# First batch's start-up order, spacing of the key/value loads, and the place of one PSUM copy in a fused attention and adapter kernel

## The chip, the cores and the metric

The kernel runs on one core of one Trainium2 chip. The metric is device time in microseconds (us) of one execution. Three timed runs of the kernel before gave 441.35, 442.04 and 440.4 us, median 441.35. One more execution was profiled; everything read from a profile below is from that one.

## What is computed

Four batches of 12288 query rows of 128 floats attend to a pooled key/value map. The map (384 x 32 positions) is averaged over 4 x 4 blocks, which gives 768 rows per batch, and multiplied by `w_sr`; keys and values are the same matrix. The attention output goes through a gated mixture of eight rank-16 adapters, of which the two with the largest logits count.

```python
kv_pool = kv.reshape(B, H // r, r, W // r, r, C).mean(axis=(2, 4))
k = v = kv_pool.reshape(B, -1, C) @ w_sr
a = softmax(scale * (q @ k.T));  x = a @ v
logits = x @ w_gate              # 8 experts, top 2, softmax over the two
out = x + sum_over_top2(w_e * ((x @ A_e) @ B_e))
```

## The kernel before, in words

**Tiling.** The 49152 query rows are 96 chunks of 512 (`NTOK`), 24 per batch (`CPB`), and four chunks form a group of 2048 rows (`GROWS`). The 768 key rows are six blocks of 128, loaded as three kv tiles per batch (`NT = 3`), each in four row parts of 512 KB.

**One order written by hand.** All instructions are emitted in program order under a manual schedule, and each engine executes its own in that order. The main loop (line 403) is a software pipeline over `c`. For the iteration `c` it emits, in this order: `scores(c+2, 0)` (TensorE product, ScalarE exponential), `gate_weights` every second iteration (ScalarE tanh, two GpSimd operations that end in `gw`), `weigh(c-1, 0)` (12 matmuls), `scores(c+2, 1)`, `up(c-5)` (four matmuls into `d_ps`, the VectorE sum `osb` at L333, and the store), `weigh(c-1, 1)`, `normalise(c-1)` (VectorE: `rinv_all`, `xn`, four MAX8 `top`), `gate` every second iteration (VectorE `msk`, GpSimd `m`, `arg`), `transposed(c-2, c-4)` (eight TensorE transposes into `t_ps`, and their copy `xh`, on VectorE at L311), `scores(c+2, 2)`, the batch preparation `prep`, `down(c-3)` (four matmuls into `h_ps`), and `apply_gate(c-3)` (the VectorE product `hg` at L322).

**What ties the steps together.** `up(c-4)` in iteration c+1 loads `hgT` as its weights, the second half of the copy `xh` of iteration c; and it writes `d_ps`, which shares its one PSUM buffer (`ps_h`, one buffer) with the `h_ps` that `hg` of iteration c reads. So `up` waits for both `xh` and `hg`. `osb` waits for `up`. `rinv_all` waits for the last matmul of `weigh`.

**Batch preparation.** While batch b runs, `prep(b+1, k)` prepares the next one, with k the chunk's number in its batch. It issues the loads of kv tile k on SP's queue at k = 0, 1, 2 (for the first batch k = 0 is emitted ahead of the loop). The pooling sums run on GpSimd at odd k from 3 to 13. At k = 16 the six pooled blocks are transposed (`kp_ps`) and copied to `kpT` (VectorE, L161), at k = 18 the keys are made (`k_ps`, copy `kfT`, L168), at k = 20 the values (`v_ps`, copy `vext`, L176), and at k = 21 two VectorE reductions run (L196, L198).

**Queues.** SP issues, in order: the kv loads (L83), the transposing loads `qT` of a query group (`load_q`, L230, every fourth iteration, at c = 2, 6, 10, ...) and one store per chunk (L335). GpSimd issues the casting copies `q_bf` (L90), one per group in the same iterations. They share the DMA engines.

**Start.** For the first group the queries are loaded as float32 (`q0`, L96) and transposed on TensorE in four blocks (L370), each copied by ScalarE to `qT[0]` (L372) with a stride, since a partition holds four neighbouring rows. Then, for each kv tile of batch 0: VectorE sums, two transposes, `kpT`, keys (L183, L184), values (L191, L193), and the scores of chunks 0, 1 and 2. The PSUM tiles of scores, transposes, keys and values rotate through two buffers (`ps_s`).

Of the kernel before, what the change touches and what calls it, by code (L numbers as in the profile page):

```python
# [11 lines left out]
BF16 = mybir.dt.bfloat16  # L12
# [3 lines left out]
AF = mybir.ActivationFunctionType  # L16
# [5 lines left out]
def kernel(  # L22
# [10 lines left out]
    nc = tc.nc  # L33
    P = 128
# [6 lines left out]
    NTOK = 512  # L41
    NS = NTOK // P
    VW = C + E + 1
    CPB = N // NTOK
    NCH = B * CPB
# [11 lines left out]
    run = ctx.enter_context(tc.tile_pool(name="run", bufs=3))  # L57
# [12 lines left out]
    qflat = q.rearrange("b n c -> (b n) c")  # L70
# [6 lines left out]
    NT = NJ // 2  # L77

    def load_kv(b, t):
        k = kvt[b, t] = kvpool.tile([P, 4, 2, 4 * C], FP32, tag="kvt", name="kvt")  # L80
        src = kv[b].rearrange("(t h d) (w e) c -> t d h w (e c)", t=NT, d=4, e=8)
        for d in range(4):
            nc.sync.dma_start(k[:, d].rearrange("p u c -> p (u c)"), src[t, d])  # L83

    GROWS = 2048
    LEAD = 2

    def cast_q(g):
        r = slice(g * GROWS, (g + 1) * GROWS)
        nc.gpsimd.dma_start(q_bf[r], qflat[r])  # L90

    q0 = kvpool.tile([P, GROWS // NTOK, NS, C], FP32, tag="kvt", name="q0")
    for t in range(NT):
        load_kv(0, t)
        if t == 0:
            nc.sync.dma_start(q0, qflat[0:GROWS].rearrange("(k p s) c -> p k s c", p=P, s=NS))  # L96

    w_in = const.tile([P, P], FP32)
    nc.scalar.dma_start(w_in, w_sr)
# [37 lines left out]
    def sum_row(b, t, d, eng):  # L137
        v = kvt[b, t]
        eng.tensor_tensor(v[:, 0], v[:, 0], v[:, d], op=ALU.add)  # L139

    def sum_cols(b, t, eng):
        v = kvt[b, t][:, 0]
        eng.tensor_tensor(v[:, :, 0:2 * C], v[:, :, 0:2 * C], v[:, :, 2 * C:4 * C], op=ALU.add)
        eng.tensor_tensor(v[:, :, 0:C], v[:, :, 0:C], v[:, :, C:2 * C], op=ALU.add)

    def stile(name):
        return ps_s.tile([P, 2, NTOK], FP32, tag="sg", name=name)
# [16 lines left out]
    def keys(b):  # L164
        t = stile("k_ps")
        for h in range(2):
            mm(t[:, h, 0:HK], w_sr_sb, kpT[b][:, h * HK:(h + 1) * HK], start=True, stop=True)
        nc.vector.tensor_copy(kfT[b].rearrange("c (h k) -> c h k", h=2), t[:, :, 0:HK])  # L168
# [10 lines left out]
    def keys_of(b, t):  # L179

        s = slice(2 * t * P, 2 * (t + 1) * P)
        k_ps = stile("k_ps")
        mm(k_ps[:, 0, 0:2 * P], w_sr_sb, kpT[b][:, s], start=True, stop=True)  # L183
        nc.scalar.activation(kfT[b][:, s], k_ps[:, 0, 0:2 * P], AF.Copy)  # L184
# [15 lines left out]

    def prep(b, k):

        if k < NT:
            load_kv(b, k)
        if k % 2 == 1 and 3 <= k < 3 + 4 * NT:
            t, h = divmod((k - 3) // 2, 2)
            if h == 0:
                sum_row(b, t, 1, nc.gpsimd)
                sum_row(b, t, 2, nc.gpsimd)
            else:  # L210
                sum_row(b, t, 3, nc.gpsimd)
                sum_cols(b, t, nc.gpsimd)
        if k == 16:
            pooled_transposed(b, range(NJ))
        elif k == 18:
            keys(b)
        elif k == 20:
            values(b)
        elif k == 21:
            ranges(b)  # L220


    qT = {}
    tt, xps, xpair, xn, gw, gin, xT, hg, hgT, hps = {}, {}, {}, {}, {}, {}, {}, {}, {}, {}
    garg, gmsk = {}, {}
    GRP = GROWS // NTOK

    def load_q(g):
        qT[g] = qpool.tile([P, GROWS], BF16, tag="qT", name="qT")
        nc.sync.dma_start(qT[g], q_bf[g * GROWS:(g + 1) * GROWS], transpose=True)  # L230

    def scores(c, r):
        b = c // CPB
        if r == 0:
            tt[c] = ttpool.tile([P, NJ, NTOK], F16, tag="tt", name="tt")
        qc = qT[c // GRP][:, (c % GRP) * NTOK:(c % GRP + 1) * NTOK]
        sg = stile("sg")
        for k in range(2):
            j = 2 * r + k
            mm(sg[:, k], kfT[b][:, j * P:(j + 1) * P], qc, start=True, stop=True)  # L240
        nc.scalar.activation(tt[c][:, 2 * r:2 * r + 2], sg, AF.Exp, bias=0.0, scale=scale)  # L241
# [50 lines left out]
    def transposed(cx, ch):  # L292

        t_ps = ps_t.tile([P, 2, NS, P], BF16, tag="tp", name="t_ps")
        todo = []
        if chunk_ok(cx):
            hi = xn[cx].bitcast(U16)[:, :, 1:2 * C:2].bitcast(BF16)
            todo += [(0, s, hi[:, s]) for s in range(NS)]
        if chunk_ok(ch):
            todo += [(1, s, hg[ch][:, s]) for s in range(NS)]  # L300
        if not todo:
            return
        for i, (k, s, src) in enumerate(todo):
            mm(t_ps[:, k, s], src, id_bf, is_transpose=True,  # L304
               start=(i == 0), stop=(i == len(todo) - 1), skip_group_check=True)
        xh = run.tile([P, 2, NS, P], BF16, tag="xh", name="xh")
        lo, hi_ = todo[0][0], todo[-1][0] + 1
        if cx >= NCH - 2:
            nc.scalar.activation(xh[:, lo:hi_], t_ps[:, lo:hi_], AF.Copy)
        else:  # L310
            nc.vector.tensor_copy(xh[:, lo:hi_], t_ps[:, lo:hi_])  # L311
        xT[cx], hgT[ch] = xh[:, 0], xh[:, 1]

    def down(c):
        hps[c] = mtile([P, NS, P], name="h_ps")
# [3 lines left out]
    def apply_gate(c):  # L319
        hg[c] = run.tile([P, NS, P], BF16, tag="hg", name="hg")  # L320
        g = gw[c // 2][:, (c % 2) * NS:(c % 2 + 1) * NS]
        nc.vector.tensor_tensor(  # L322
            hg[c].rearrange("p s (e r) -> p (s e) r", r=RK),
            hps[c].rearrange("p s (e r) -> p (s e) r", r=RK),
            g.rearrange("p s e -> p (s e)").unsqueeze(2).broadcast_to([P, NS * E, RK]),
            op=ALU.mult)
# [10 lines left out]
    def chunk_ok(c):  # L337
        return 0 <= c < NCH
# [25 lines left out]


    qT[0] = qpool.tile([P, GROWS], BF16, tag="qT", name="qT")
    for k in range(GRP):
        t = stile("q_ps")
        for i in range(NS):
            mm(t[:, 0, i * P:(i + 1) * P], q0[:, k, i], id_f32, is_transpose=True,  # L370
               start=(i == 0), stop=(i == NS - 1), skip_group_check=True)
        nc.scalar.activation(  # L372
            qT[0][:, k * NTOK:(k + 1) * NTOK].rearrange("c (p s) -> c s p", s=NS),
            t[:, 0].rearrange("c (s p) -> c s p", s=NS), AF.Copy)

    a_bf = const.tile([P, P], BF16)
    b_half = const.tile([P, P], FP32)
# [1 line left out]
    for t in range(NT):  # L379
        for d in range(1, 4):  # L380
            sum_row(0, t, d, nc.vector)
        sum_cols(0, t, nc.vector)
        pooled_transposed(0, [2 * t, 2 * t + 1])
        if t == 0:
            nc.vector.tensor_copy(a_bf, a_f)
            nc.vector.tensor_scalar(b_half, b_f, 0.5, None, op0=ALU.mult)
            nc.vector.tensor_copy(b_bf, b_half)
        if t == NT - 1:
            tick = const.tile([P, 1], FP32)
            nc.gpsimd.tensor_copy(tick, kvt[0, t][:, 1, 0, 0:1])  # L390
            for g in range(1, 4):
                cast_q(g)
        keys_of(0, t)
        scores(0, t)
        values_of(0, t)
        for c in range(1, LEAD + 1):
            scores(c, t)
    load_q(1)
    load_q(2)
    prep(1, 0)  # L400

    NQ = NCH // GRP
    for c in range(1, NCH + 5):
        b, k = divmod(c, CPB)
        cs = c + LEAD
        if cs < NCH:
            if cs % GRP == 0:
                g = cs // GRP
                if g + 2 < NQ:
                    load_q(g + 2)  # L410
                if g + 3 < NQ:
                    cast_q(g + 3)
            scores(cs, 0)
        if chunk_ok(c - 2) and (c - 2) % 2 == 1:
            gate_weights((c - 2) // 2)
        if chunk_ok(c - 1):
            weigh(c - 1, 0)
        if cs < NCH:
            scores(cs, 1)
        if chunk_ok(c - 5):  # L420
            up(c - 5)
        if chunk_ok(c - 1):
            weigh(c - 1, 1)
            normalise(c - 1)
            if (c - 1) % 2 == 1:
                gate((c - 1) // 2)
        transposed(c - 2, c - 4)
        if cs < NCH:
            scores(cs, 2)
        if c < NCH:  # L430
            if b + 1 < B:
                prep(b + 1, k)
            if c == 1:
                ranges(0)
        if chunk_ok(c - 3):
            down(c - 3)
            apply_gate(c - 3)
        if c == NCH + 1:
            direct_ok()

# [3 lines left out]
    with tc.If(bad_v != 0):  # L444
# [8 lines left out]
        for b in range(B):  # L453
            for h in range(2):
                s = slice(h * NKV // 2, (h + 1) * NKV // 2)
# [104 lines left out]
```

## Time and profile before

| what | value |
|---|---|
| timed runs, median | 441.35 us |
| the profiled execution, its own time | 444.76 us |
| its span, first to last instruction | 443.0 us |
| what lies around the span | 1.76 us |
| busy: TensorE matmul / VectorE / ScalarE / GpSimd | 385.4 / 345.6 / 294.9 / 165.8 us |
| mean granted TensorE clock | 0.974 |

The profile gives, for each group of instructions, how long they were busy, how long one took, and what ended the idle time before them. The chain of waits follows the last instruction back, at each step to what released it. The timeline lists start, duration, engine, line and names; a bracket gives the idle time of the engine before the row and its releaser. "PE" is TensorE's matmul, "PEld" its weight load, "DVE" VectorE, "ACT" ScalarE, "POOL" GpSimd, "SP" SyncE. "issue" is idle time for which the profile shows no releaser.

### The profile page before, as it was taken

To read this page: it belongs to the slowest core of one execution; us is meant where nothing else is said; L and a number is where in the kernel's file an instruction comes from. 1 tells how busy PE (TensorE), PEld (TensorE's weight loads), DVE (VectorE), ACT (ScalarE), POOL (GpSimd) and SP (SyncE) were. 2 spreads that over 40 slices of the span, in tenths; PEclk is the share of its full clock that TensorE was granted. 3 is DMA by queue.
4 is the path that set the end of the run, shared out by engine and by line. 5 is a ranking of instruction groups with operands and counts; after the bars stand their busy time and mean duration, and the time that the engine had idled before them with its cause. 6 is when DMAs were issued, how large, how long until landed. Compare 5 with 4: busy or idle time off the path is not lost.

```text
span 443.0 us, 11324 instructions
## 1 busy us (share of the span) xinstructions
PE 385.4 (87%) x4455; PEld 302.6 (68%) x4527; DVE 345.6 (78%) x967; ACT 294.9 (67%) x351; POOL 165.8 (37%) x317
## 2 busy tenths in 40 slices
PE   0678996999989999999989999999989999999742
PEld 0335774777867777777877777777877777777641
DVE  3473786588888888888888888888888888888882
ACT  1468875677667777776667777767667777777321
POOL 1100886461122678752121787832113121121210
PEclk9989999799999999999999999999999999999995
DMA  8999999764466999685388999677357444111112
GB/s 269 405 201 280 308 175 177 152 144 97 144 124 209 321 288 234 161 168 115 102 167 225 284 279 243 175 155 144 102 119 164 117 122 121 73 66 59 70 72 78
DMA packets 71372, 76.51 MB, mean 173 GB/s; under 512 B 51744, under 2 KB 52000, under 8 KB 70944
## 3 DMA queue, kind: packets, MB, share of 16 engines
q1 hardware_dynamic: 69104, 63.45, 52.6%
q0 software_dynamic: 736, 12.06, 15.9%
q8 instruction: 37, 0.61, 0.6%
q10 hardware_dynamic: 1472, 0.20, 0.3%
q14 instruction: 23, 0.19, 0.2%
HBM read 50.53 MB, written 37.22 MB: 198 GB/s over the span
## 4 chain that ended last, share of the span: by engine, by line
PE 60%; DVE 29%; issue 4%; ACT 3%; DMA 3%; SPq 1%; DVEq 0%; ACTq 0%
PE xps L250 22%; PE sg L240 15%; DVE xh L311 9%; DVE hg L322 9%; PE d_ps L331 8%; PE t_ps L304 7%; PE h_ps L317 6%; DVE xn L261 5%; DMA q<-in_q_dram 2%; DVE top L268 2%; ACT tt L241 2%; DVE rinv_all L257 1%; PE v_ps L174 1%; PE k_ps L183 1%; ACT qT L372 1%
## 5 line engine op out<-in xcount | busy, mean ns | idle before, releaser
L241 ACT ACTIVATE tt<-sg 128x1024 f16<-128x1024 f32 x288 | 280.7, 1023 | 107.2 <-PE sg L240 75.9
L250 PE MATMUL xps<-vext,tt 128*128 128x137 f16 x2304 | 171.7, 224 | 2.0 <-DVE xn L261 0.7
L250 PEld LDWEIGHTS <-tt 128*128 128x128 f16 x2304 | 154.8, 113 | 23.6 <-DVE xn L261 2.3
L240 PE MATMUL sg<-qT,kfT 128*128 128x512 bf16 x504 | 158.2, 386 | 8.0 <-issue 4.1
L333 DVE TENSOR_TENSOR osb<-d_ps,xn 128x512 f32<-128x512 f32 x96 | 66.4, 692 | 48.2 <-PE d_ps L331 48.2
L274 POOL TENSOR_TENSOR m<-top 128x8 f32<-128x8 f32 x48 | 11.4, 237 | 183.5 <-DVE top L268 183.5
L261 DVE TENSOR_TENSOR xn<-xps,rinv_all 128x548 f32<-128x548 f32 x96 | 69.9, 728 | 3.3
L322 DVE TENSOR_TENSOR hg<-h_ps,gw 128x512 bf16<-128x512 f32 x96 | 65.3, 680 | 5.0 <-PE h_ps L317 5.0
L139 POOL TENSOR_TENSOR kvt<-kvt 128x1024 f32<-128x1024 f32 x27 | 64.0, 2369 | 0.7
L331 PEld LDWEIGHTS <-xh 128*128 128x128 bf16 x384 | 29.6, 98 | 49.4 <-issue 35.0
L311 DVE COPY xh<-t_ps 128x1024 bf16<-128x1024 bf16 (+1 forms) x94 | 63.1, 672 | 0.0
L331 PE MATMUL d_ps<-b_bf,xh 128*128 128x128 bf16 x384 | 37.6, 221 | 20.1 <-DVE hg L322 19.2
L240 PEld LDWEIGHTS <-kfT 128*128 128x128 bf16 x576 | 45.6, 99 | 13.1 <-issue 9.4
L317 PEld LDWEIGHTS <-xh 128*128 128x128 bf16 x384 | 29.7, 99 | 21.8 <-issue 2.2
L317 PE MATMUL h_ps<-a_bf,xh 128*128 128x128 bf16 x384 | 37.5, 221 | 2.0 <-DVE osb L333 0.7
L268 DVE MAX8 top<-xn 128x8 f32<-128x8 f32 x384 | 35.9, 156 | 3.3
L304 PE MATMUL t_ps<-id_bf,hg 128*128 128x128 bf16 x384 | 37.6, 221 | 0.0
L304 PE MATMUL t_ps<-id_bf,xn 128*128 128x128 bf16 x384 | 37.1, 219 | 0.0
L289 POOL TENSOR_SCALAR th<-th 128x64 f32<-128x64 f32 x48 | 17.8, 370 | 48.9 <-ACT th L287 48.9
L257 DVE RECIPROCAL rinv_all<-xps 128x4 f32<-128x4 f32 x96 | 17.5, 183 | 13.4 <-PE xps L250 10.1
L304 PEld LDWEIGHTS <-xn 128*128 128x128 bf16 x384 | 26.0, 98 | 0.0
L304 PEld LDWEIGHTS <-hg 128*128 128x128 bf16 x384 | 25.9, 99 | 0.0
(67 smaller groups left out, 186.5 us busy)
## 6 DMA issues: line engine op xcount, KB each, us to landing
kvt<-in_kv_dram SPq DMA_DIRECT2D x48, 512.0 KB, 7.2
out_dram<-osb SPq DMA_DIRECT2D x96, 256.0 KB, 3.0
q_bf<-in_q_dram POOLq DMA_DIRECT2D x23, 512.0 KB, 6.8
q<-in_q_dram SPq DMA_DIRECT2D x1, 1024.0 KB, 9.7
qT<-q_bf SPq DMA_TRANSPOSE x23, 8.4
w_in<-in_w_sr_dram ACTq DMA_DIRECT2D x1, 64.0 KB, 1.8
a_f<-in_moe_A_dram ACTq DMA_DIRECT2D x1, 64.0 KB, 10.2
b_f<-in_moe_B_dram ACTq DMA_DIRECT2D x1, 64.0 KB, 10.7
```

Source lines behind the costliest of these rows:

```text
L139: eng.tensor_tensor(v[:, 0], v[:, 0], v[:, d], op=ALU.add)
L240: mm(sg[:, k], kfT[b][:, j * P:(j + 1) * P], qc, start=True, stop=True)
L241: nc.scalar.activation(tt[c][:, 2 * r:2 * r + 2], sg, AF.Exp, bias=0.0, scale=scale)
L250: mm(o, tt[c][:, j, s::NS], vext[b][:, j], start=(j == 0 and s % 2 == 0), stop=(j == NJ - 1 and s % 2 == 1), skip_group_check=True)
L261: nc.vector.tensor_tensor(xn[c].rearrange("p (b s) v -> p b s v", b=2), xv, ri.rearrange("p (b s) -> p b s", b=2).unsqueeze(3).broadcast_t ...
L268: nc.vector.max(gin[c // 2][:, (c % 2) * NS + s], xn[c][:, s, C:C + E])
L304: mm(t_ps[:, k, s], src, id_bf, is_transpose=True, start=(i == 0), stop=(i == len(todo) - 1), skip_group_check=True)
L311: nc.vector.tensor_copy(xh[:, lo:hi_], t_ps[:, lo:hi_])
L317: mm(hps[c][:, s], xT[c][:, s], a_bf, start=(s == 0), stop=(s == NS - 1))
L322: nc.vector.tensor_tensor(hg[c].rearrange("p s (e r) -> p (s e) r", r=RK), hps[c].rearrange("p s (e r) -> p (s e) r", r=RK), g.rearrange(" ...
L331: mm(d_ps[:, s], hgT[c][:, s], b_bf, start=(s == 0), stop=(s == NS - 1))
L333: nc.vector.tensor_tensor(osb, d_ps, xn[c][:, :, 0:C], op=ALU.add)
```

## The change

There are three parts. **Start:** `q0` is loaded with each partition holding rows 128 apart (2048 runs of 512 bytes in place of 512 runs of 2 KB), so that its copy to `qT[0]` is contiguous. The transposes of the first kv tile come before the query blocks, and each query block comes just ahead of the first scores that need it; the fourth comes after all three kv tiles. **Loads:** the kv loads of the next batch move from k = 0, 1, 2 to k = 2, 6, 10, their sums to k = 5 to 15, and the pooled transposes from k = 16 to k = 17; keys, values and reductions stay. **Gate product:** the copy `xh` is emitted at the end of the iteration, so that on VectorE it stands behind the `prep` copies and behind `hg`.

```diff
-            nc.sync.dma_start(q0, qflat[0:GROWS].rearrange("(k p s) c -> p k s c", p=P, s=NS))
+            nc.sync.dma_start(q0, qflat[0:GROWS].rearrange("(k s p) c -> p k s c", p=P, s=NS))
...
-        if k < NT:
-            load_kv(b, k)
-        if k % 2 == 1 and 3 <= k < 3 + 4 * NT:
...
-        if k == 16:
+        if k in (2, 6, 10):
+            load_kv(b, (k - 2) // 4)
+        if k in (5, 9, 13):
+            sum_row(b, (k - 5) // 4, 1, nc.gpsimd)
+            sum_row(b, (k - 5) // 4, 2, nc.gpsimd)
+        elif k in (7, 11, 15):
+            sum_row(b, (k - 7) // 4, 3, nc.gpsimd)
+            sum_cols(b, (k - 7) // 4, nc.gpsimd)
+        if k == 17:
             pooled_transposed(b, range(NJ))
...
-        xh = run.tile([P, 2, NS, P], BF16, tag="xh", name="xh")
...
+        def evacuate():
+            xh = run.tile([P, 2, NS, P], BF16, tag="xh", name="xh")
...
+        return evacuate
...
-        nc.scalar.activation(
-            qT[0][:, k * NTOK:(k + 1) * NTOK].rearrange("c (p s) -> c s p", s=NS),
-            t[:, 0].rearrange("c (s p) -> c s p", s=NS), AF.Copy)
+        nc.scalar.activation(qT[0][:, k * NTOK:(k + 1) * NTOK], t[:, 0], AF.Copy)
...
         keys_of(0, t)
+        if t == 0:
+            queries(0)
         scores(0, t)
         values_of(0, t)
         for c in range(1, LEAD + 1):
+            if t == 0:
+                queries(c)
             scores(c, t)
+    for k in range(LEAD + 1, GRP):
+        queries(k)
     load_q(1)
     load_q(2)
-    prep(1, 0)
...
-        transposed(c - 2, c - 4)
+        evacuate = transposed(c - 2, c - 4)
...
             down(c - 3)
             apply_gate(c - 3)
+        evacuate()
```

More of the change, by code (lines that the diff above doesn't have):

```diff
@@ L201, in prep @@
     def prep(b, k):
-        if k < NT:
-            load_kv(b, k)
-        if k % 2 == 1 and 3 <= k < 3 + 4 * NT:
[L206 to L212, printed above, removed]
-        if k == 16:
+        if k in (2, 6, 10):
[7 more added lines that the diff above has]
+        if k == 17:
             pooled_transposed(b, range(NJ))
@@ L301, in transposed @@
         if not todo:
-            return
+            return lambda: None
         for i, (k, s, src) in enumerate(todo):
@@ L305, in transposed @@
                start=(i == 0), stop=(i == len(todo) - 1), skip_group_check=True)
-        xh = run.tile([P, 2, NS, P], BF16, tag="xh", name="xh")
[L307 to L312, printed above, removed]
+        def evacuate():
+            xh = run.tile([P, 2, NS, P], BF16, tag="xh", name="xh")
+            lo, hi_ = todo[0][0], todo[-1][0] + 1
+            if cx >= NCH - 2:
+                nc.scalar.activation(xh[:, lo:hi_], t_ps[:, lo:hi_], AF.Copy)
+            else:
+                nc.vector.tensor_copy(xh[:, lo:hi_], t_ps[:, lo:hi_])
+            xT[cx], hgT[ch] = xh[:, 0], xh[:, 1]
+        return evacuate
     def down(c):
@@ L366, with queries @@
     qT[0] = qpool.tile([P, GROWS], BF16, tag="qT", name="qT")
-    for k in range(GRP):
+    def queries(k):
         t = stile("q_ps")
```

## The prediction

> **What bounds the kernel now.** I read the chain of waits first, then the groups, then the timeline of one ordinary iteration, and last the DMA view by stretches. From the page:
>
> ```profile
> PE 60%; DVE 29%; issue 4%; ACT 3%; DMA 3%; SPq 1%; DVEq 0%; ACTq 0%
> ...
> L333 DVE TENSOR_TENSOR osb<-d_ps,xn 128x512 f32<-128x512 f32 x96 | 66.4, 692 | 48.2 <-PE d_ps L331 48.2
> L322 DVE TENSOR_TENSOR hg<-h_ps,gw 128x512 bf16<-128x512 f32 x96 | 65.3, 680 | 5.0 <-PE h_ps L317 5.0
> ```
>
> The chain runs mostly over PE, but it is a loop of PE and DVE: DVE's only large idle time is 48.2 us ahead of `osb`, 0.47 us in each of some 95 iterations. The timeline of an iteration with a gate shows the loop (start, duration, engine):
>
> ```profile
> 96.23 0.23 DVE L278 TENSOR_TENSOR msk<-xn,top 128x64 f32<-128x64 f32 x1
> ...
> 96.37 0.69 DVE L311 COPY xh<-t_ps 128x1024 bf16<-128x1024 bf16 x1
> ...
> 96.97 0.68 DVE L322 TENSOR_TENSOR hg<-h_ps,gw 128x512 bf16<-128x512 f32 x1
> 97.12 0.10 PEld L331 LDWEIGHTS <-xh 128*128 128x128 bf16 x1
> ...
> 97.71 0.38 PE L331 MATMUL d_ps<-b_bf,xh 128*128 128x128 bf16 x4 [0.21 <-DVE hg L322]
> ...
> 98.13 0.69 DVE L333 TENSOR_TENSOR osb<-d_ps,xn 128x512 f32<-128x512 f32 x1 [0.47 <-PE d_ps L331]
> ```
>
> DVE runs `osb`, `rinv_all`, `xn`, `top`, (`msk`), `xh`, `hg` without a break, then waits 0.47 us for `up` (L331), which waits for it. The starts of `rinv_all` give the period: 94.84, 98.86, 102.60, that is 4.02 us with a gate and 3.74 without. **Whatever lengthens DVE's loop counts fully; whatever PE, ACT or POOL lose inside their slack counts nothing.**
>
> **Gate product first, ordinary iterations.** `up` needs `xh` (weights) and `hg` (PSUM buffer), so their order moves no end: the later one still releases `up`. But the later one is now the weights. Above, the first weight load starts at 97.12, 0.06 after `xh`, and is done long before `hg` ends; in the new order it comes after the last wait. The nearest row for an exposed load is a `weigh` whose weight load itself waited, beside one whose load ran ahead:
>
> ```profile
> 44.04 0.75 PEld L250 LDWEIGHTS <-tt 128*128 128x128 f16 x12 [0.44 <-DVE xn L261]
> 44.04 0.92 PE L250 MATMUL xps<-vext,tt 128*128 128x137 f16 x12
> ...
> 45.01 0.94 PEld L250 LDWEIGHTS <-tt 128*128 128x128 f16 x12
> ...
> 45.23 0.89 PE L250 MATMUL xps<-vext,tt 128*128 128x137 f16 x12
> ```
>
> From the release to the last matmul's end 0.92 against 0.89: 0.03 us. Of the 96 `up`, some 92 follow a DVE copy: 92 x 0.031 = **+2.9 us**. Bounds: -0.9 (a weight load started 0.05 after its release, a matmul 0.06) and +9.0 (92 x 0.098, the mean L331 load in full). I take the row's own 0.03. `hg` now needs `h_ps` 0.6 us sooner, and has it: in that stretch `h_ps` (95.52, 0.39) ends at 95.91 and `msk` at 96.46; without a gate the slack is 0.29 us (99.53 + 0.39 = 99.92 against `top`'s end at 100.21). `gw` ends at 98.67, over a microsecond ahead of the 100.13 at which `hg` would want it.
>
> [...]
>
> **Gate product first, preparation iterations.** Here `xh` covered DVE's wait for the preparation's matmuls. The keys' iteration:
>
> ```profile
> 111.90 1.45 PE L167 MATMUL k_ps<-kpT,w_sr_sb 128*128 128x384 f32 x4
> ...
> 112.61 0.23 DVE L278 TENSOR_TENSOR msk<-xn,top 128x64 f32<-128x64 f32 x1
> ...
> 112.75 0.68 DVE L311 COPY xh<-t_ps 128x1024 bf16<-128x1024 bf16 x1
> ...
> 113.39 0.96 DVE L168 CAST kfT<-k_ps 128x768 bf16<-128x768 f32 x1
> ...
> 114.27 0.68 DVE L322 TENSOR_TENSOR hg<-h_ps,gw 128x512 bf16<-128x512 f32 x1
> ```
>
> `k_ps` ends at 113.35, so `kfT` can't start before 113.39 in either order. Before, `xh` filled DVE from 112.75; now DVE idles there and `xh` comes later: +0.60 (its effective 0.6, as its successor overlaps its tail). The values alike: `v_ps` ends at 122.13, `vext` starts at 122.17, `xh` had run 121.43 to 122.11: +0.60. The pooled copy: `kp_ps` ends at 104.10, 0.15 after `top` (103.95); at k = 17 there is no `msk`, so `kpT` starts at +0.19 in place of -0.08: +0.27. The reductions wait for no matmul. Per batch 1.47, three batches: **+4.4 us**. Bounds: 0 (a wait can't become a gain) and 6.1 (nine copies at 0.68).
>
> **Start.** Before, the last row of kv tile 0 is summed at 13.10, but PE transposes queries from 13.15 (when `q0` has landed) and reaches the tile only at 18.19, 5.06 us late. The first block then runs to the next tile's transposes at 25.43. Now the tile goes at 13.13, but three query blocks stand inside the block, one after the other with the scores, since two PSUM buffers rotate. By before's rows (transposes 1.13; copy contiguous about 0.6, estimated between the 0.38 for 256 and the 1.02 for 1024 columns on ACT; scores 1.05; exponential 1.03): keys copied 16.05, first query block ready 17.15, first exponential ends 19.3; second block ready 21.1, exponential 23.2; third ready 23.85, exponential 26.0. The second tile's keys follow at 26.05 in place of 26.48: -0.43. The fourth query block adds 0.6 on ACT, where seven exponentials run back to back (36.33 for 7.00 us): **about 0**. Bounds: -4.5 (the 5.06 kept, less 0.6) and +1.5. The 512-byte runs of `q0` may land later; the cover is from 13.1 to 15.4, when PE first wants them. If it lands after that, each microsecond costs one in this block.
>
> **Loads.** The profile has one hole, in batch 0:
>
> ```profile
> 73.19 0.39 PE L304 MATMUL t_ps<-id_bf,hg 128*128 128x128 bf16 x4
> 77.68 0.58 PE L240 MATMUL sg<-qT,kfT 128*128 128x512 bf16 x1 [4.11 <-issue]
> ```
>
> PE stands 4.11 us with no releaser, then runs on half the clock (granted 0.66 from 73.2 to 83.3). `rinv_all` shows 10.17 us where 4.0 is due: 6.2 us lost. The DMA view by stretches says why. From 40 to 53 us the queue of kind "instruction" (q8) moved two packets; from 53 to 75 none; at 75 to 78 one, and PE went on:
>
> ```profile
> q1 hardware_dynamic: 2872, 3.03, 95.8%
> q0 software_dynamic: 20, 0.52, 18.3%
> ...
> qT<-q_bf SPq DMA_TRANSPOSE x1, 22.1
> ```
>
> That is 53 to 75: a transposing load, queued behind kv tile 2 and mixed with a casting copy, took 22.1 us (median 8.4). PE's instructions came late. Now kv tile 0 goes behind `load_q(3)`, and at c = 6 `load_q(4)` starts on a clear queue, with the cast a few microseconds later on POOL (behind 4.82 us of sums). I expect no such jam: **-6.2 us** in this execution; 0 if it recurs. [...]
>
> The price to pay is lead: all nine tiles now have three iterations (11.6 us) from `prep`'s load to the sums, and stand on SP behind a transposing load (issue 1.3 to 12.1 us, median 4.8) and a store. About 5 + 3 of issue and up to 5 to land leave it just in time; POOL's slack (1.4 us at `gw`, 0.6 at `m`) is the cover. I take 0; bounds 0 and +9 (nine tiles, 1 us each).
>
> **Sum**, on the profiled execution: 444.76 + 2.9 + 4.4 + 0 - 6.2 = 445.9 us. That execution is 3.4 us above the median of the timed runs. Nearly every period outside the hole repeats to 0.02 us, so part of the 3.4 may be the hole itself, shorter when not profiled. If all of it, the timed runs can win only 2.8: 441.35 + 7.3 - 2.8 = 445.9. If none: 441.35 + 1.1 = 442.5. I weigh the first 0.6: **444.5 us**.
>
> **Rivals.** *The hole stays or was never in the timed runs* (0.20): 441.35 + 7.3 = 448.7. For it: the same bytes must move in the same 40 us. Against: batches 1 and 2 mix the same loads without a hole. *The start keeps its lead* (0.12, the other side): if PE's query transposes hide between the exponentials and the first block keeps 4.5 of its 5.06 us, with the hole wholly gone: 441.35 + 7.3 - 6.2 - 4.5 = 437.9. It is faster than measurement error from a lead of 3.3 us on. Against it: each block waits for its PSUM buffer. *POOL waits for kv rows* (0.10): the gate then delays `hg`; at 5 us net, 441.35 + 7.3 - 2.8 + 5 = 450.9. My own case has 0.58, from 442.5 to 445.9.
>
> A measurement of this kernel can tell about 0.5% (2.2 us) from no change: 439.1 to 443.6. My case gives 0.20 to "same" and 0.38 to "slower"; the first and third rivals are slower, the second faster: 0.12, 0.20, 0.68. The range 440.0 to 449.5 leaves out the second rival and most of the third.
>
> **What would show it.** Right: `osb`'s idle time at 0.50, with the L331 weight load released by `xh`; periods 3.77 and 4.05; DVE idle ahead of L168 and L176, of 0.5 to 0.6 us; no "issue" gap of PE over 1 us; second tile's keys near 26. Wrong: periods unchanged, POOL idle behind kv rows at the sums with `hg` waiting for `gw`, or the second tile's keys before 23.

## The result, and the profile after

The changed kernel takes 445.71 us (median; 442.53 to 448.59) against 440.40 us (438.30 to 446.61) for the kernel before on the same chip: a ratio of 1.0121, 95% interval 1.0089 to 1.0153. It is slower by 5.3 us. An execution over 1.5% above the fastest of its kernel (here the 446.61) is left out of the ratios, so that these are not quite the quotients of the medians, and of the spreads compared further below. The profiled execution took 446.5 us, its span is 444.7 us.

The page of the changed kernel; a group's line gives busy time, mean ns of one, then the idle time ahead of it and what ended most of that:

```profile
PE 61%; DVE 27%; DMA 5%; issue 3%; ACT 2%; SPq 0%; DVEq 0%; ACTq 0%
...
L334 DVE TENSOR_TENSOR osb<-d_ps,xn 128x512 f32<-128x512 f32 x96 | 66.4, 692 | 47.6 <-PE d_ps L332 47.6
...
L323 DVE TENSOR_TENSOR hg<-h_ps,gw 128x512 bf16<-128x512 f32 x96 | 65.2, 679 | 1.2 <-PE h_ps L318 1.2
...
L332 PEld LDWEIGHTS <-xh 128*128 128x128 bf16 x384 | 22.2, 98 | 62.6 <-DVE xh L310 58.8
```

The chain is still the loop of PE and DVE. What changed is the last line: the weight load of `up` (L332) waits 58.8 us for `xh`. DVE's copy is now the later of the two things that release `up`. Before, most of the idle time ahead of the same load has no releaser ("issue"):

```profile
L331 PEld LDWEIGHTS <-xh 128*128 128x128 bf16 x384 | 29.6, 98 | 49.4 <-issue 35.0
```

The total ahead of `osb` fell, 48.2 to 47.6, and misleads: before's 48.2 holds 2.3 us of the hole (the same kernel without it, profiled again, has 45.9).

The waits of the changed kernel (us in total, times, longest):

```profile
engine line waited for: us in total, times, longest us
...
DVE osb L334 <- PE d_ps L332: 47.6, 95, 1.1
...
DVE vext L176 <- PE v_ps L174: 2.0, 3, 0.7
...
DVE kfT L168 <- PE k_ps L167: 1.7, 3, 0.6
...
POOL kvt L139 <- DMA kvt<-in_kv_dram: 1.3, 2, 0.9
```

DVE now waits for the values' and the keys' matmuls, three times each, one per prepared batch; the waits of before have neither line. POOL waits for key/value rows twice, 1.3 us in all: the loads come late enough to be seen. It costs little: beside one of the two late sums `msk` takes 0.38 us for its usual 0.23, and that period is 4.19 us for 4.03.

The timeline of the keys' iteration and the ordinary one behind it (start, duration, engine; in brackets idle time and releaser):

```profile
109.33 0.96 DVE L168 CAST kfT<-k_ps 128x768 bf16<-128x768 f32 x1 [0.55 <-PE k_ps L167]
...
110.21 0.68 DVE L323 TENSOR_TENSOR hg<-h_ps,gw 128x512 bf16<-128x512 f32 x1
...
110.81 0.68 DVE L310 COPY xh<-t_ps 128x1024 bf16<-128x1024 bf16 x1
...
111.98 0.69 DVE L334 TENSOR_TENSOR osb<-d_ps,xn 128x512 f32<-128x512 f32 x1 [0.49 <-PE d_ps L332]
...
115.30 0.23 PEld L332 LDWEIGHTS <-xh 128*128 128x128 bf16 x4 [0.44 <-DVE xh L310]
115.31 0.40 PE L332 MATMUL d_ps<-b_bf,xh 128*128 128x128 bf16 x4
...
115.74 0.69 DVE L334 TENSOR_TENSOR osb<-d_ps,xn 128x512 f32<-128x512 f32 x1 [0.49 <-PE d_ps L332]
```

DVE stands 0.55 us ahead of `kfT`, where before it ran `xh`; then `kfT`, `hg` and `xh` follow in a row, and `osb` waits 0.49 us in either iteration (0.47 before). By the starts of `rinv_all`, ordinary iterations take 3.76 and 4.03 us (3.74 and 4.01 before), the keys' 5.54 (4.93), the values' 5.69 (5.08).

I split a span at the starts of the first and the last `rinv_all`, into a start, a loop, and 18.4 to 18.8 us of end. The start went from 39.92 to 41.94, the loop from 384.43 to 384.19. The loop looks unchanged, and is not: before's held the 6.2 us hole, which the changed kernel's lacks, so 6 us went in elsewhere.

### The profile page after: what moved, and what is told of

The parts are those of the page before. It is cut to its first block, busy times and chain, and to the rows that moved or that the text cites. A ratio compares the mean times of both kernels' runs of the same rounds, so it can differ in the third digit from the quotient of the medians.

```text
span 444.7 us, 11323 instructions
## 1 busy us (share of the span) xinstructions
PE 386.5 (87%) x4455; PEld 295.6 (66%) x4527; DVE 345.7 (78%) x967; ACT 292.2 (66%) x351; POOL 165.4 (37%) x317
## 4 chain that ended last, share of the span: by engine, by line
PE 61%; DVE 27%; DMA 5%; issue 3%; ACT 2%; SPq 0%; DVEq 0%; ACTq 0%
PE xps L248 22%; PE sg L238 16%; DVE hg L323 10%; DVE xh L310 8%; PE d_ps L332 8%; PE t_ps L302 7%; PE h_ps L318 5%; DVE xn L259 3%; DMA qT<-q_bf 3%; DMA kvt<-in_kv_dram 2%; DVE top L266 1%; ACT tt L239 1%; PE v_ps L174 1%; DVE rinv_all L255 1%; DVE vmax L196 1%
## 5 line engine op out<-in xcount | busy, mean ns | idle before, releaser
L334 DVE TENSOR_TENSOR osb<-d_ps,xn 128x512 f32<-128x512 f32 x96 | 66.4, 692 | 47.6 <-PE d_ps L332 47.6
L332 PEld LDWEIGHTS <-xh 128*128 128x128 bf16 x384 | 22.2, 98 | 62.6 <-DVE xh L310 58.8
L332 PE MATMUL d_ps<-b_bf,xh 128*128 128x128 bf16 x384 | 38.7, 224 | 24.4 <-DVE xh L310 20.9
L318 PEld LDWEIGHTS <-xh 128*128 128x128 bf16 x384 | 29.5, 98 | 21.5 <-issue 1.7
```

Source lines behind the costliest of these rows:

```text
L318: mm(hps[c][:, s], xT[c][:, s], a_bf, start=(s == 0), stop=(s == NS - 1))
L332: mm(d_ps[:, s], hgT[c][:, s], b_bf, start=(s == 0), stop=(s == NS - 1))
L334: nc.vector.tensor_tensor(osb, d_ps, xn[c][:, :, 0:C], op=ALU.add)
```

## Theory and rival

*Theory:* the gate part costs 5 to 6 us, by the lost cover at preparation copies and the exposed weight load; start and loads are worth about nothing, and the hole was an accident of one execution. *Rivals:* the gate part costs only its weight load, some 1.8 us, and the rest is the start, which is 2 us later in the changed profile; or the loads do take a real hole out, and the gate part costs more than its waits show.

## Experiments: one part at a time

Times are compared with the kernel before on the same chip: 440.98 us for e1 to e4, 439.49 for e5 to e8, 439.69 for e9 to e11.

**e1: before, with the gate part alone.**

```diff
...
-        transposed(c - 2, c - 4)
+        evacuate = transposed(c - 2, c - 4)
...
             apply_gate(c - 3)
+        evacuate()
```

> The kernel before with the gate-product part alone: the copy xh behind the preparation's copies and behind hg. Theory (the prediction's): 0.02 us in each of 92 iterations (the period rose from 3.74 to 3.76 and from 4.02 to 4.04 in the profile of the changed kernel) and 1.47 us per batch preparation, 4.4 in all; sum +6.2 us, ratio 1.014. Rival: the order costs only what ordinary iterations show, +1.8 us, ratio 1.004, and the rest of the loss comes from the start. The profile should show DVE waiting 0.5 to 0.7 us ahead of L168 and L176.

446.14 us, ratio 1.0129 (1.0078 to 1.0180). Periods 3.76 and 4.03, preparation iterations 4.91, 5.54, 5.69, loop 383.6 us. The gate part alone brings the whole slowdown: its loop is 5.4 us longer than that of the kernel before without the hole (e8, below). It still has the old loads, and no hole.

**e2: before, with the start part alone.**

```diff
...
         keys_of(0, t)
+        if t == 0:
+            queries(0)
         scores(0, t)
...
+            if t == 0:
+                queries(c)
             scores(c, t)
...
```

> The kernel before with the start part alone. Theory from the changed kernel's profile: the first chunk's rinv_all comes 2.0 us later (41.9 against 39.9), because the fourth query block stands behind all three kv tiles and TensorE falls to half its clock there; so +2.0 us, ratio 1.005. The prediction had 0, and its second rival -4.5. The hole of PE in batch 0 may stand or go with it: the loads are as before.

441.47 us, ratio 1.0011 (0.9976 to 1.0047): nothing that can be measured. In its profile the first `rinv_all` comes at 43.95, 4 us later than before, and the loop takes 378.3 us: again old loads and no hole.

**e3: before, with the loads part alone.**

```diff
-        if k < NT:
-            load_kv(b, k)
+        if k in (2, 6, 10):
+            load_kv(b, (k - 2) // 4)
...
```

> The kernel before with the spacing of the kv loads alone, and the pooled transposes at k = 17. Theory: no hole of PE in the profile, so -6.2 us against the profiled execution of before; in the timed runs, whose median of 440.4 is 4.4 under that execution, -2 us, ratio 0.995. Rival: the hole is an accident of one execution, so the loads are worth 0 in the timed runs, and a hole can also come here.

438.75 us, ratio 0.9973 (0.9944 to 1.0003). Loop 378.1 us, first `rinv_all` at 39.01. That is some 1.2 us less, and the interval, from 2.5 us less to 0.1 more, takes in none. The profile shows one iteration of batch 0 that became shorter, 4.02 us for 4.56. Before, VectorE's `msk` met one of GpSimd's pooling sums there:

```profile
46.61 4.82 POOL L139 TENSOR_TENSOR kvt<-kvt 128x1024 f32<-128x1024 f32 x2
...
50.74 0.77 DVE L278 TENSOR_TENSOR msk<-xn,top 128x64 f32<-128x64 f32 x1
```

`msk` took 0.77 us in place of 0.23, and ended 0.08 us after the sum. With the new spacing no sum runs at that place.

**e4: the changed kernel without the gate part.**

```diff
-        evacuate = transposed(c - 2, c - 4)
+        transposed(c - 2, c - 4)()
...
-        evacuate()
```

> The changed kernel with xh copied at once again, so start and loads alone. Theory: the changed kernel less 6.2 us, 439.5 us, ratio 0.998 to before; periods back at 3.74 and 4.02, and the preparation iterations at 4.6, 4.9, 5.1, 4.7. Rival (the order costs 1.8 alone): 443.9, ratio 1.008.

438.72 us, ratio 0.9982 (0.9942 to 1.0021). Loop 378.07 against 384.19 us with the gate part: 6.12 us by the profiles.

**e5: the changed kernel, `xh` ahead of the preparation in its three iterations.**

```diff
+                if k in (17, 18, 20):
+                    evacuate()
+                    evacuate = lambda: None
                 prep(b + 1, k)
```

> The changed kernel, but in the three iterations of a batch whose preparation makes DVE wait for PE (pooled rows, keys, values) the copy xh goes ahead of the preparation again; all other iterations keep the gate product first. The theory puts +1.47 to 1.5 us per batch, 4.4 us in all, on the copy having lost DVE's wait as its cover, and the rest of the gate order, 92 x 0.019 = 1.75 us, on the exposed weight load. It expects: preparation iterations back near 4.70 (pooled), 4.95 (keys), 5.10 (values), ordinary periods still 3.76 and 4.03, and from first to last rinv_all about 379.8 us (384.2 in the changed kernel, 378.1 with the gate part undone); a time about 4.4 us under the changed kernel's 445.7, so some 441, and a ratio to the kernel before of 1.000 to 1.003. The rival, that the order costs its time through something else (POOL, the stores, hg's earlier end), expects no change in the preparation iterations and a time of 444 to 446, ratio about 1.012.

440.58 us, ratio 1.0036 (1.0006 to 1.0065). Preparation iterations 4.69, 4.93, 5.08, loop 379.66 us. DVE in its keys' iteration:

```profile
105.51 0.68 DVE L310 COPY xh<-t_ps 128x1024 bf16<-128x1024 bf16 x1
106.14 0.96 DVE L168 CAST kfT<-k_ps 128x768 bf16<-128x768 f32 x1
107.02 0.68 DVE L323 TENSOR_TENSOR hg<-h_ps,gw 128x512 bf16<-128x512 f32 x1
```

`kfT` has no bracket: the copy stands where the wait was. That splits the 6.12 us: 384.19 - 379.66 = 4.53 for the lost cover, 379.66 - 378.07 = 1.59 for the rest, which the waits of L332 put at the weight loads. The first rival falls.

**e8: the kernel before, unchanged, profiled again.**

> The kernel before, unchanged, profiled a second time. The question is the hole of batch 0: 4.11 us in which PE waits for nothing that the profile shows, with 6.2 us lost in one step of rinv_all. If the hole belongs to the kernel, it recurs: span near 443, first to last rinv_all near 384.5. If it is an accident of that one execution, no gap of PE with no releaser is over 1 us, the step of that iteration is 4.0, and first to last rinv_all is 378.3, as in the two kernels that have the same loads and showed none.

Span 436.3 us, loop 378.25. PE around the place of the hole:

```profile
72.54 0.39 PE L304 MATMUL t_ps<-id_bf,xn 128*128 128x128 bf16 x4
72.76 0.39 PE L304 MATMUL t_ps<-id_bf,hg 128*128 128x128 bf16 x4
72.98 0.38 PE L240 MATMUL sg<-qT,kfT 128*128 128x512 bf16 x1
```

The scores follow the transposes at once, where the first profile had 4.11 us of nothing. The same two transfers went faster: the casting copy landed 12.1 us after its issue (19.5), the transposing load 15.5 us (22.1). The hole is an accident of one execution; e1, e2 and e9, with the same loads, have none either. What made it isn't shown: in e8 too the instruction queue moved nothing from 52 to 69 us, and PE went on.

## Experiments: the start with PE's clock held

Two kernels with the same start order (before at 39.92, e1 at 42.37) and two with the new one (e4 at 40.28, e2 at 43.95) lie further apart than the orders do. So e6, e7 and e9 to e11 add matmuls, of which nothing reads the result, to PE's idle time in the start:

```diff
...
+    def warm(n):
+        t = mtile([P, NTOK], name="warm_ps")
+        for _ in range(n):
+            mm(t, id_bf, warm_in, start=True, stop=True)
+    warm(22)
...
         keys_of(0, t)
+        warm(2)
...
         scores(0, t)
+        warm(2)
...
             scores(c, t)
+            warm(2)
```

**e6: the loads part alone, with these (and `warm(2)` behind each query block).**

> The kernel before with the loads part alone, and with extra matmuls (128x512, bf16) put into PE's idle time in the start, so that PE is busy throughout; they write a PSUM buffer that nothing reads. Theory: what swings the start from run to run (first rinv_all at 39.0 to 44.0 us in six profiles) is PE's clock, which drops to half after idle stretches. It expects a granted clock near 1.0 from about 20 us on, the first rinv_all at 37 us or sooner (39.0 with the loads part alone), and a time 1 to 2.5 us under the loads part alone (438.75). Rival: the start is bound by ACT's copies and exponentials and by the landing of the rows; then the extra matmuls only stand in the way, the first rinv_all stays at 39 or comes up to 2 us later, and the time is that of the loads part alone or up to 2 us more.

436.50 us (435.94 to 438.15), ratio 0.9931 (0.9906 to 0.9955); first `rinv_all` at 37.75, not quite the 37 expected.

**e7: e4 with these, and the fourth query block behind the second kv tile.**

```diff
+        if t == 1:
+            queries(LEAD + 1)
-    for k in range(LEAD + 1, GRP):
-        queries(k)
```

> The changed kernel with the gate part undone, with the same extra matmuls in the start, and with the fourth query block's transposes put right behind the second kv tile's blocks, and not behind the third's. Theory: the start part keeps the lead of its first tile (keys at 24.07 for 26.48 us) only if PE's clock holds and the fourth query block doesn't stand at the end; then the first rinv_all comes at 36 to 37 us (40.3 without these two), and the time is 435 to 437, ratio about 0.99. Rival: the start's order is worth nothing, since ACT's 0.6 us for each query block is the same wherever it stands; then the first rinv_all stays near 39 to 40 and the time near 438.7, ratio about 0.998.

436.22 us (435.73 to 436.77), ratio 0.9917 (0.9885 to 0.9950); first `rinv_all` at 37.50, between the two expectations. This is the fastest version, ahead of both kernels; from e6 it can't be told apart.

**e9, e10, e11: before, the whole change, and the change without the gate part, all with these matmuls** (in e9 also behind each query block).

> The kernel before with the extra matmuls in the start and nothing else (they write a PSUM buffer that nothing reads). It gives the loads part its price with the clock held: against the same kernel with the loads part (436.5 us). Theory: the loads part is worth the 0.5 us of one iteration (4.56 to 4.02) and no more, so this takes some 437, with a spread under 3 us; if the 4.11 us hole of one profile belonged to the timed runs of the kernel before, the time would be 439 to 442.7 here, since the old loads are still in it.

> The whole change with the extra matmuls in the start. Theory: with the clock held, the gate part is what is left of the difference: first to last rinv_all 384.2, first rinv_all at 37.5 to 38.5, and a time 5.3 to 6.2 us over the same kernel without the gate part, some 442 to 443.5. Rival: part of the changed kernel's 445.7 is an interplay of the gate order with the start; then the difference to the kernel without the gate part is clearly under 5 or over 7.

> The changed kernel with the gate part undone and the extra matmuls in the start, the fourth query block still last in the start. Against the loads part alone with the same matmuls (436.5) it prices the start part with the clock held. Theory: the order of the start is worth nothing, since ACT's copies and exponentials are the same work; first rinv_all within 0.7 us of 37.7, time 436 to 437.2. Rival: the lead of 2.4 us that the second kv tile's keys showed is kept once the clock is held: first rinv_all near 35.5, time near 434.

| kernel | us, median (range) | ratio to before (95%) |
|---|---|---|
| e9, before | 437.11 (436.36 to 437.71) | 0.9931 (0.9907 to 0.9954) |
| e11, change without the gate part | 437.05 (436.08 to 437.77) | 0.9929 (0.9904 to 0.9954) |
| e10, whole change | 442.48 (441.65 to 443.20) | 1.0057 (1.0034 to 1.0081) |

The runs of each of the five kernels with extra matmuls lie within 2.2 us, where those of the kernel before range over 4.0 to 5.2 us, by chip (437.99 to 441.99, 437.84 to 443.03). Start and loads together: -0.06 us. The gate part: +5.43 us. e9, with the old loads in it, takes no 439 to 442.7, so the second rival falls too.

**What the clock does.** PE in the start of e2, then of e11 with the extra matmuls:

```profile
25.23 1.22 PE L183 MATMUL k_ps<-kpT,w_sr_sb 128*128 128x256 f32 x2 [0.52 <-DVE kpT L161]
26.93 1.03 PE L240 MATMUL sg<-qT,kfT 128*128 128x512 bf16 x2 [0.48 <-ACT kfT L184]
27.75 1.11 PE L191 MATMUL v_ps<-wext,kpT 128*128 128x136 f32 x4
```

```profile
24.03 0.67 PE L183 MATMUL k_ps<-kpT,w_sr_sb 128*128 128x256 f32 x2 [0.61 <-DVE kpT L161]
```

The same product takes 1.22 us in the one and 0.67 in the other. Over all profiles:

| kernel | mean of one scores matmul, 14 to 38 us | first `rinv_all` |
|---|---|---|
| e7, e6, e10, e11, e9 (extra matmuls) | 379 to 380 ns | 37.50, 37.75, 37.99, 38.33, 38.74 |
| e3 | 440 | 39.01 |
| e4, e5, before, e8 | 474, 498, 500, 501 | 40.28, 39.08, 39.92, 39.49 |
| changed kernel | 530 | 41.94 |
| e2, e1 | 616, 619 | 43.95, 42.37 |

So most of the start's swing, from 37.5 to 44 us, is PE's clock: e2 and e11 have the same order of the start, and their first `rinv_all` comes at 43.95 and 38.33. e2's row by stretches (PE busy, PEld, DVE, ACT, POOL, then granted clock) doesn't show it:

```profile
28.00:32.00 4.00, 3.42 (x10) 1.28 (x9) 2.02 (x4) 3.19 (x4) 0.00 (x0) 1.00 1.25 263
```

It says 1.00 while e2's scores matmuls take 616 ns (mean) for the 379 of e11: the trace of e2 has no clock record before 42.8 us, where they fall from 631 to 380 ns, and the column reads 1.00 where there is none. The durations of like matmuls are the surer reading: two scores matmuls of e2 take 1.04 us at 34.16 and four query transposes 1.12 at 38.43, as in the changed kernel where its records say 0.50 (1.01 at 37.28, 1.11 at 35.48). The records of before and of the changed kernel show half clock, ahead of the kernel's end, in stretches of 3.41, 6.83 and 10.24 us.

In before's hole, where PE stands from 73.57 to 77.68 us, the records turn to half clock at 75.55 and back to full at 82.37. In the five profiles with extra matmuls, the first of which runs at about 7 us, the durations turn to those of full clock 2.8 to 4.6 us after it. First `rinv_all` at 43.95 for 38.33 is 5.6 us, 1.3% of the span, in the slowest start that was profiled.

**What the new order of the start does**, clock held. ScalarE in e6 (old order), then in e11 (new):

```profile
31.35 0.38 ACT L184 ACTIVATE kfT<-k_ps 128x256 bf16<-128x256 f32 x1 [1.08 <-PE k_ps L183]
...
34.13 7.02 ACT L239 ACTIVATE tt<-sg 128x1024 f16<-128x1024 f32 x7 [0.39 <-PE v_ps L191]
```

```profile
30.55 0.38 ACT L184 ACTIVATE kfT<-k_ps 128x256 bf16<-128x256 f32 x1 [1.09 <-PE k_ps L183]
...
35.16 0.60 ACT L383 ACTIVATE qT<-q_ps 128x512 bf16<-128x512 f32 x1
36.44 5.29 ACT L239 ACTIVATE tt<-sg 128x1024 f16<-128x1024 f32 x5 [0.68 <-PE sg L238]
```

At the third tile's keys the new order leads by 0.80 us. The extra matmuls stand in its way by 0.67 (first kv tile's transposes at 13.79, 13.12 in the changed kernel) and in e6's by 0.27 (queries landed at 12.87, transposed at 13.14), so the lead itself is some 1.2. The fourth query block then takes 1.28 back: 0.60 copied, 0.68 waiting for the scores behind it, where e6 runs its exponentials in a row. e7 moves that block into the middle, and its first `rinv_all` is 0.25 ahead of e6's. e9's extra matmuls held its queries back by 1.1 us (landed 13.02, transposed 14.14), so its price, and any price of the start, is good to 1 us only.

## Why the prediction was right, and where not

Forecast 444.5 us, its own sum 445.9; the runs gave 445.71. The sign and the mechanism of the gate part are confirmed. That the sum agrees so closely is in part luck: a cost (the weight load, by 1.3 us) and a gain (the loads, by 2.6 us) were both too large, and the loads' mechanism was wrong.

- **"Gate product first, preparation iterations", +4.4: right.** 4.53 us by e5. Keys and values +0.61 each (0.60 forecast), pooled rows +0.22 (0.27), 4.32 in the nine iterations. The pooled rows' part needs the copy at k = 17, as in the loads part: in e1, at k = 16, that iteration takes 4.91 us for 4.88. The wait of 0.55 ahead of `kfT` is where it was put.
- **"Gate product first, ordinary iterations", +2.9: mechanism right, size too large.** `xh` releases `up` 92 times, as forecast; the price is at most e5's remaining 1.59 us, 0.017 each, not 0.031. It was taken from a row of another shape (12 `weigh` matmuls of 137 columns); `up`'s own rows, four matmuls with the load exposed and without, are 0.40 and 0.38 us. A mean L331 load in full, 0.098 us each (the upper bound, +9.0), is over five times too much: in the rows at 115.30 and 115.31 above, the first load and the first matmul start 0.01 us apart.
- **"Start", 0: right in the sum, wrong in the terms.** "The second tile's keys follow at 26.05": 24.07 in the changed kernel. The working took transposes at 1.13 and scores at 1.05 us, both from rows at half clock; from 18.5 to 25.4 us this execution's clock was full, and they took 0.66 and 0.59. In e2, at half clock by the durations up to 42.8 us, it is 25.23, still 0.8 sooner than forecast. "The fourth query block adds 0.6 on ACT": 1.28 in e11, since the scores behind the copy have to wait for it. `q0` in 512-byte runs landed at 14.12 us (13.11 before), inside the cover that was named. In the changed kernel's profile the first `rinv_all` is 2.0 us later than before, with half clock up to 18.5 by the durations and in 13.2 of the 23.4 us behind it by the records; in the timed runs nothing is left (e2 1.0011, e11 against e9 -0.06 us).
- **"Loads", -6.2, weighed to -2.8 in the timed runs: the step that failed.** The transfers were slow in that stretch, as read; that they held up PE's instructions was argued and no run shows it, and to take the hole for a property of the kernel's order was wrong. e8 has the same order, the same casting copy at the same place, and no hole. Loop 378.25 in e8, 378.10 in e3: the loads part is worth 0.15 us. One iteration gains 0.54 (4.56 to 4.02, where `msk` met the sum), and the pooled copy loses 0.09 per batch in its new iteration (4.69 for 3.74 at k = 17, 4.88 for 4.02 at k = 16).
- **The sum.** From the median: +4.5 + 1.6 - 0.2 + 0 = 5.9, the runs have 5.3, and 5.4 with the clock held. The forecast's own case had 441.35 + 4.5; the median it started from was itself 1 us above the longer series.
- **Rivals.** "The hole stays or was never in the timed runs" (448.7) had the right mechanism, and missed by the weight load and that starting median. "The start keeps its lead": some 1.2 of 5.06 us, and spent again. "POOL waits for kv rows": it does, 1.3 us in the changed kernel, but not by the path named, since `gw` is ready 0.48 us or more ahead of every `hg`, in all profiles. A late sum counts where `msk` meets it: 0.16 us in the changed kernel, 0.80 in e11 (one period of 4.82 us for 4.02, `msk` 1.04 us). In all eight profiles in which `msk` meets such a sum, it ends 0.08 to 0.09 us after it; why isn't shown.

Left open: whether the slowest timed runs of the kernel before (446.6, 447.8) hold such a hole. None of them was profiled; a start with PE at half clock can make several microseconds too (e2's first `rinv_all` for e11's: 5.6). Open too is what stopped PE in the hole.

## What to carry to other kernels

A copy that looks early in an engine's order may be the cover of a wait; before moving it behind other work, find each place where the next instruction is not yet ready, for those iterations pay up to the whole copy (0.6 us here) while the others pay hundredths. An irregular stall seen once in a profile gets no credit before a second profile of the same kernel shows it. Where a start-up's times swing, compare the durations of like matmuls first; extra matmuls that hold the clock were worth more (0.7%) than the reordering of start and loads (nothing that could be measured).

## What was not expected of the hardware

- Extra matmuls that nobody reads make the kernel before 0.69% faster (0.46% to 0.93%), and its runs then lie within 1.4 us, not 4.0.
- Two executions of one program differ by 6.6 us in the time of one transposing load beside a casting copy (22.1 and 15.5 us, issued at 55 and 54 us), and one of them leaves PE without a releaser for 4.11 us. In that one the instruction queue moved nothing from 53 to 75 us; in the other it moved two packets.
- The granted clock column reads 1.00 where the trace has no clock record, up to 42.8 us into an execution (e2) whose scores matmuls took 616 ns (mean, 14 to 38 us) and 380 behind it.
- A VectorE operation on 128x64 values takes 0.23 us, and 0.38 to 1.04 us where it meets a pooling sum of GpSimd, whose end it outlasts by 0.08 to 0.09 us.
